# Bucketed attention and a gated product: queries and keys split to float16 in token order and turned by DMA, in place of TensorE transposes and float32r scores

## The chip, the cores and the metric

The kernel runs on one core of one Trainium2 chip. The metric is device time in microseconds (us): the median of the runs of one launch. A core has TensorE (PE; its weight loads are listed as PEld), VectorE (DVE), ScalarE (ACT), GpSimd (POOL) and SyncE (SP), which here only issues DMAs, all on one queue. The hash, score and product matmuls accumulate in PSUM.

## The reference, cut to what matters

```python
batch, n_heads, seq, head_dim = (4, 8, 768, 64)
...
q_bits = (np.einsum('bhsd,dk->bhsk', q, proj) > 0).astype(np.int64)
k_bits = (np.einsum('bhsd,dk->bhsk', k, proj) > 0).astype(np.int64)
powers = 2 ** np.arange(n_bits)
q_bucket = np.sum(q_bits * powers, axis=-1)
k_bucket = np.sum(k_bits * powers, axis=-1)
mask = q_bucket[:, :, :, None] == k_bucket[:, :, None, :]
scores = scale * np.matmul(q, k.transpose(0, 1, 3, 2))
scores = np.where(mask, scores, -1000000000.0)
...
x = np.ascontiguousarray(attn_out.transpose(0, 2, 1, 3)).reshape(B * S, H * D)
...
a = x @ w_a
b = x @ w_b
return (a * b @ w_out).astype(np.float32)
```

Each query and key is hashed to 6 bits by the signs of its products with `proj`; a query sees only the keys of its own bucket of 64. After softmax and the product with v, the heads are laid side by side as x (3072 x 512), which goes through w_a and w_b (512 x 1536 each) and w_out (1536 x 512). The weights arrive as float64, the rest as float32.

## The kernel before, in words

**Work.** There are 4 batches, each of 3 chunks of 256 queries and 2 halves of 4 heads: 24 score units of 8 tiles. A tile is 128 queries of one head against all 768 keys. `qtile` (line 730) makes a tile: scores on TensorE (L740), the maximum on VectorE (L752), a bias (L759), the exponential on ScalarE (L767), a float16 high part of the weights of attention by a cast (L776 on ScalarE for the first eight tiles, L781 on VectorE after), the low part by a subtraction on GpSimd (L786), a DMA transpose of both parts at once (L792), and 18 small matmuls with the high and low parts of v (L801). `su_end` divides by the sums and transposes the unit into the float16 pair xT. `moe` (line 858) takes a chunk of 256 tokens through w_a and w_b (L885: high and low float16 parts, three products), multiplies the two (L899, L907, L914, L917) and runs w_out in float32r (L927); its result is stored at L944.

**Keys and queries.** `kprep` (line 519) loads a pair of heads with tokens and heads interleaved in pieces of 256 bytes (L530), transposes six blocks of 128 x 128 on TensorE (L539), and evicts each head's 64 rows as float32r: high part by ScalarE (L548), a copy of it by GpSimd (L555), low part by VectorE (L560). `bit_rows` (L513) then multiplies by the six hash columns, in two passes for the first batch. The signs become bits (L581, L595), a matmul (L604) turns bits into a distance from each of the 64 buckets, and ScalarE writes a penalty into the 64 unused rows (L613). `qprep` (line 620) does the same for 4 heads of a chunk of queries (L630, L644, L654, L659, L664, L513, L683, L696, L705, L714), with a one-hot row in place of the penalty. So 128 rows hold 64 of data and 64 of marks, and two products a tile give high x high with the mask, and the crossed terms with the low parts.

**Weights.** `to_f32` (line 342) loads a piece of 128 x 512 float64 numbers as pairs of 32-bit words, scales the exponent of the upper word and takes the top byte of the lower one on ScalarE (L355, L363), and joins them to float32 on VectorE (L370). `w_group` (line 377) does so for the four pieces of 512 columns of w_a or w_b (6 groups), takes their common maximum (L400), makes a power of two of it (`scale_of`, L312 to L329), and splits into float16 high (L420, ScalarE) and low (L425, VectorE). `wo_piece` (line 431) does the 12 pieces of w_out (L436, L439). Pieces land in buffers that w_out's products take later.

**Order.** Nothing runs in the order of the source. Every operation is put into a list with its engine, a duration, a key (when it is due, counted in tiles) and the buffers it uses; `Plan.issue` (line 141) then walks through a modelled time and gives each engine the ready operation with the least key whose buffers are free. What comes out is a fixed order for each engine and for SyncE's queue, with waits between them. Keys come from constants: `K0`, `V0`, `Q0`, `WG0`, `WO0`, `M0` for the first batch, weights and first two chunks of the product, `K_LEAD`, `Q_LEAD`, `V_LEAD`, `M_LAG` for the rest.

## Time and profile before

| | |
|---|---|
| median of 3 runs | 1012.9 us (1012.79 to 1012.94) |
| span of the profiled execution | 1010.4 us; its own time is not given beside it, and the medians of the runs lie 2.5 us above |
| TensorE, VectorE, ScalarE, GpSimd busy | 936.4, 630.5, 557.5, 456.2 us |
| DMA | 127.46 MB moved, its queue busy 54.9% of the span |
| chain that ended last | TensorE 86%, VectorE 7%, ScalarE 3% |

The span runs from the first to the last instruction. A busy TensorE is not one at its peak, since matmuls overlap and their ends are modelled; so where matmuls are packed, their cost is read from the start of one group to the start of the next. A row of the groups gives line, engine, operation, written and read tiles, shapes and count, then busy us and mean ns, then idle us before it and what ended that.

### The profile page before, as it was taken

How to read it: one execution, taken by the hardware profiler on the slowest of the kernel's cores; microseconds unless marked ns; L12 is line 12 of the kernel's file. 1: busy time of each engine (PE TensorE's matmuls, PEld its weight loads, DVE VectorE, ACT ScalarE, POOL GpSimd, SP SyncE). 2: the span in 40 equal slices, each digit the busy share in tenths (PEclk: the TensorE clock that was granted, in tenths of full speed). 3: DMA queues.
4: the chain of work that ended last, by engine and by line, in shares of the span. 5: the costliest groups of instructions: out<-in, count | busy, mean ns of one | idle time of the engine just before them, and what ended most of it. 6: DMA issues, size and time to landing. Idle time of an engine off the chain costs nothing.

```text
span 1010.4 us, 22786 instructions
## 1 busy us (share of the span) xinstructions
PE 936.4 (93%) x9132; PEld 793.3 (79%) x9132; DVE 630.5 (62%) x1135; ACT 557.5 (55%) x1067; POOL 456.2 (45%) x372
## 2 busy tenths in 40 slices
PE   3464679999999999999999999999999999999998
...
GB/s 286 223 213 208 188 127 139 123 165 149 102 124 116 105 101 131 110 131 152 119 128 106 105 127 109 108 149 137 126 123 103 105 133 103 95 101 95 32 22 21
DMA packets 370154, 127.46 MB, mean 126 GB/s; under 512 B 353920, under 2 KB 362368, under 8 KB 370048
## 3 DMA queue, kind: packets, MB, share of 16 engines
q1 hardware_dynamic: 370048, 126.00, 54.9%
...
## 4 chain that ended last, share of the span: by engine, by line
PE 86%; DVE 7%; ACT 3%; issue 2%; DMA 1%; SPq 0%; POOL 0%; POOLq 0%; DVEq 0%; ACTq 0%
PE ab L885 37%; PE o L927 19%; PE s L740 13%; PE av L801 9%; PE kb L513 2%; PE qb L513 2%; DVE mx L752 1%; PE pk L539 1%; PE px L837 1%; PE pq L644 1%; ACT e L767 1%; DVE wab L370 1%; DVE wab L425 1%; DVE trk L560 1%; PE ko L604 1%
## 5 line engine op out<-in xcount | busy, mean ns | idle before, releaser
L786 POOL TENSOR_TENSOR a<-e,a 128x768 f16<-128x768 f32 x192 | 323.2, 1683 | 322.0 <-DVE a L781 175.9
L885 PE MATMUL ab<-xT,wab 128*128 128x256 f16 x3456 | 413.3, 273 | 0.5 <-DVE bias L759 0.5
L885 PEld LDWEIGHTS <-wab 128*128 128x128 f16 x3456 | 326.4, 98 | 59.4 <-issue 23.3
L767 ACT ACTIVATE e<-s,bias 128x768 f32<-128x768 f32 x192 | 172.7, 899 | 136.5 <-DVE bias L759 125.1
L927 PE MATMUL o<-wo,g 128*128 128x512 f32 x864 | 234.3, 406 | 0.3 <-ACT g L914 0.2
L752 DVE TENSOR_REDUCE mx<-s 128x1 f32<-128x768 f32 x192 | 182.5, 951 | 70.1 <-PE s L740 69.2
L917 POOL TENSOR_TENSOR g<-g,g 128x256 fp32r<-128x256 f32 x144 | 109.0, 757 | 186.1 <-ACT g L914 175.2
L740 PE MATMUL s<-trk,trq 128*128 128x384 f32 x768 | 180.5, 365 | 7.8 <-ACT e L767 6.3
L927 PEld LDWEIGHTS o<-wo,g 128*128 128x128 f32 x864 | 153.4, 189 | 27.6 <-ACT g L914 0.7
L907 DVE SCALAR_TENSOR_TENSOR g<-ab,absc,a 128x256 f32<-128x256 f32 x144 | 69.4, 482 | 158.8 <-ACT a L899 147.1
L801 PEld LDWEIGHTS <-at 128*128 128x128 f16 x3456 | 122.7, 100 | 32.7 <-issue 24.0
L740 PEld LDWEIGHTS s<-trk,trq 128*128 128x128 f32 x768 | 135.5, 198 | 15.7 <-ACT e L767 10.5
L899 ACT ACTIVATE a<-ab,absc 128x256 f32<-128x256 f32 x144 | 68.3, 474 | 131.0 <-PE ab L885 129.9
L801 PE MATMUL av<-vh,at 128*128 128x64 f16 x2304 | 133.8, 196 | 4.8 <-DMA at<-a 4.8
L781 DVE CAST a<-e 128x768 f16<-128x768 f32 x184 | 111.5, 606 | 25.7 <-ACT e L767 19.6
L914 ACT CAST g<-g 128x256 fp32r<-128x256 f32 x144 | 58.1, 404 | 55.9 <-DVE g L907 54.1
L801 PE MATMUL av<-vl,at 128*128 128x64 f16 x1152 | 66.6, 195 | 1.8 <-DVE vl L499 1.8
L714 ACT ACTIVATE trq<-qo,csb 64x512 fp32r<-64x512 f32 x48 | 32.8, 683 | 35.4 <-PE qo L705 34.9
L664 DVE TENSOR_TENSOR trq<-pq,trq 64x512 fp32r<-64x512 f32 x48 | 33.0, 688 | 24.2 <-ACT trq L659 20.7
L555 POOL CAST trk<-trk 64x768 fp32r<-64x768 f32 x32 | 26.7, 833 | 40.3 <-ACT trk L548 39.4
L560 DVE SCALAR_TENSOR_TENSOR trk<-pk,trk 64x768 fp32r<-64x768 f32 x32 | 30.6, 955 | 21.7 <-ACT trk L548 21.2
L654 ACT CAST trq<-pq 64x512 fp32r<-64x512 f32 x48 | 27.8, 580 | 23.0 <-PE pq L644 20.0
...
## 6 DMA issues: line engine op xcount, KB each, us to landing
...
```

The source lines that it names most:

```text
L740: nc.tensor.matmul(ps.t[:, jj, :HALF], lhsT=trq.t[:, j, i, t * P : (t + 1) * P], rhs=tr.t[:, i, jj * HALF : (jj + 1) * HALF], start=i == 0 ...
L752: lambda: nc.vector.tensor_reduce(out=mx.t[:, u : u + 1], in_=halves(ps.t), axis=AX.XY, op=ALU.max, negate=True),
L767: lambda: nc.scalar.activation(flat2(e.t), halves(ps.t), AF.Exp, bias=bias.t[:, u : u + 1], scale=1.0, accum_out=sm.t[:, u : u + 1],),
L781: "DVE", 0.55, lambda: nc.vector.tensor_copy(out=a2.t[:, 0], in_=e.t), key,
L786: lambda: nc.gpsimd.tensor_tensor(out=a2.t[:, 1], in0=e.t, in1=a2.t[:, 0], op=ALU.subtract),
L801: nc.tensor.matmul(av.t[:, u, :], lhsT=at.t[:, a + kt, :], rhs=w.t[:, h, kt, :], start=i == 0, stop=i == 3 * NT - 1,)
L885: nc.tensor.matmul(pl.t[:, m, :CH], lhsT=wt(m, wi, cc, f), rhs=xi.t[:, cc, :], start=i == 0, stop=i == 3 * NC - 1,)
L899: lambda a=a, pl=pl, gr=gr: nc.scalar.activation(a.t, pl.t[:, 0, :CH], AF.Copy, scale=absc[:, b, gr : gr + 1]),
L907: lambda a=a, g32=g32, pl=pl, gr=gr: nc.vector.scalar_tensor_tensor(out=g32.t, in0=pl.t[:, 1, :CH], scalar=absc[:, b, gr + 1 : gr + 2], in ...
L914: op("ACT", 0.41, lambda g=g, g32=g32: nc.scalar.copy(out=g[0].t, in_=g32.t), kf - 8, r=[g32], w=[g[0], "order_g0"])
L917: lambda g=g, g32=g32: nc.gpsimd.tensor_tensor(out=g[1].t, in0=g32.t, in1=f32(g[0].t), op=ALU.subtract),
L927: nc.tensor.matmul(po.t[:, u, :], lhsT=g[gi].t[:, us], rhs=wo[f].t[:, wi * DM : (wi + 1) * DM], start=f == 0 and i == 0, stop=f == NF - 1 ...
```

## The change

- **Queries and keys stay in token order.** A key unit is a pair of heads in 12 blocks of 128 tokens, a query unit a whole chunk of all 8 heads in 16 blocks. `split` makes a float16 high part (ScalarE), a copy (GpSimd) and a low part (VectorE) beside each other in blocks of 128 x 128: B holds high and low, A holds high and, later, marks. Both are scaled by a power of two: the keys by one for the batch (`k_scale`, which loads all keys of the batch once more, except in the first), the queries by one a chunk for each partition.
- **Turning.** `turn` transposes B and then A, by DMA transposes on SyncE's queue; for the first batch's keys and its first chunk of queries by TensorE, with an eviction on ScalarE (B) or VectorE (A).
- **Hash.** `buckets` multiplies each turned block of B, as the weight, by 12 columns (high and low parts of `proj`), so the bits of a token lie in one partition. VectorE adds the parts, tests the sign, sums to a bucket number, and compares it with 0 to 63 for the marks in A. A second buffer of A does not exist (nA has one, nB two).
- **Scores** are four float16 matmuls of 384 columns. The exponential's scale undoes the powers of two, so a second small VectorE operation a tile sets it (`affine`). Every third tile of a unit is cast on ScalarE.
- **Weights.** The maximum is taken over the upper words as they land, the scale goes into ScalarE's `Prelu`, the high part is a plain copy, and the low parts of the weights and of w_out move from VectorE to GpSimd.
- **Plan.** New constants; four buffers in place of two for the attention weights before and after their transpose; a key and value pair of the first batch is loaded once, into buffers that are used for other things later; buffers of some kinds are now taken in the order in which they were made (`IN_TURN`).

The diff, cut to its core:

```diff
-NE, NA, NAT, NO = 3, 2, 2, 2
...
+NE, NA, NAT, NO, NRAW = 3, 4, 4, 2, 2
...
+ACT_CASTS = 8.63
+CAST_EVERY = 3
+K_LEAD, KS_LEAD, Q_LEAD, V_LEAD = 16.63, 10.65, 7.77, -17.89
+M_LAG = 6.32
+KS0 = -2.53
+K0 = [-63.42, -14.05, -9.5, 14.86]
+V0 = [-11.8, -2.03, 6.24, -14.06]
+Q0 = [-60.96, 10.19, 23.45]
+VS0 = -1.83
+WG0 = [3.31, -0.76, 4.06, 8.52, 14.53, 16.59]
+WO0 = [14.19, 25.61, 30.83]
+M0 = [20.43, -64.42]
+M0_PACE = [2.33, 2.19]
+NBLK = NH * TPC
+HOT = 65504.0
...
         fq, m = g // 2, g % 2
-        zs = []
+        raws = []
+        mx = buf("wmx", [P, NC + 1], F32, f"wmx{g}")
         for cc in range(NC):
             k = g * NC + cc
-            if k + 1 < NPC:
-                tok = ("W", k + 1)
-                z = lambda k=k: wab[:, k + 1, :]
+            src = (w_a, w_b)[m][cc * P : (cc + 1) * P, fq * WP : (fq + 1) * WP]
+            raw = words(src, NF - NSTG + k % NSTG, f"w{k}", key + 0.5 * cc)
+            raws.append(raw)
+            op(
+                "DVE", 0.6,
+                lambda raw=raw, cc=cc: nc.vector.tensor_reduce(
+                    out=mx.t[:, cc + 1 : cc + 2], in_=raw.t[:, :, 1].bitcast(F32), axis=AX.X, op=ALU.max,
+                    apply_absolute_value=True,
+                ),
+                key + 0.5 * cc, r=[raw], w=[(mx, cc)],
+            )
+        key += 0.5 * NC
+        op(
+            "DVE", 0.15,
+            lambda: nc.vector.tensor_reduce(out=mx.t[:, 0:1], in_=mx.t[:, 1:], axis=AX.X, op=ALU.max),
+            key, r=[(mx, cc) for cc in range(NC)], w=[mx],
+        )
+        sc = buf("wsc", [P, 1], F32, f"wsc{g}")
+        w_scale(mx, sc, winv[:, g : g + 1], ("winv", g), f"w{g}", key)
...
+            to_f32(raw, NF - NSTG + k % NSTG, key, z, [tok], sc, [sc, (mx, cc)])
             hi, lo = wab16[:, k, :WP], wab16[:, k, WP:]
             op(
-                "ACT", 0.74,
-                lambda hi=hi, z=z: nc.scalar.activation(hi, z(), AF.Copy, scale=sc.t),
-                key, r=[ztok, sc], w=[("W", k)],
-            )
-            op(
-                "DVE", 0.75,
-                lambda hi=hi, lo=lo, z=z: nc.vector.scalar_tensor_tensor(
-                    out=lo, in0=z(), scalar=sc.t, in1=hi, op0=ALU.mult, op1=ALU.subtract
-                ),
...
-            "DVE", 0.7,
-            lambda: nc.vector.tensor_tensor(
+            "POOL", 1.15,
+            lambda: nc.gpsimd.tensor_tensor(
                 out=wo[f].t[:, DM:], in0=y.t, in1=f32(wo[f].t[:, :DM]), op=ALU.subtract
             ),
-            key, r=[y, (wo[f], 0)], w=[(wo[f], 1)], sbuf=True,
-        )
...
+    HOME0 = [(f"wo{i}", 1, cp) for i in range(4)] + [("a2", NA, p2)] * 2 + [("at", NAT, p2)] * 2
...
+    def k_scale(b, key):
+        ksc[b] = buf("ks", [P, 1], F32, f"ks{b}")
+        largest(
+            k, b, ksc[b], kinv[:, b : b + 1], ("kinv", b), f"k{b}", key,
+            None if b else k0, least=1.0, top=QK,
+        )
...
+    def buckets(tB, n, pw, a, op_eq, value, name, key, tag):
+        ps = psum(f"b_{name}", tag)
+        def rows():
+            for u in range(n):
                 nc.tensor.matmul(
-                    out[:m], lhsT=pjw[:, w0 + lo : w0 + lo + m], rhs=rhs,
-                    start=i == 0, stop=i == len(groups) * len(passes) - 1,
+                    ps.t[:, 0, u * 2 * NBITS : (u + 1) * 2 * NBITS], lhsT=tB.t[:, u, :],
+                    rhs=pw.rearrange("p a b -> p (a b)"), start=True, stop=True,
                 )
-                i += 1
+        op("PE", 0.03 * n, rows, key, r=[tB, "pjk", "pjq"], w=[ps])
+        sums = buf("b_sum", [P, NBITS * NBLK], F32, f"bs_{name}")
+        code = buf("b_code", [P, NBLK, 2], F16, f"bc_{name}")
+        def codes():
+            s = sums.t[:, : NBITS * n]
+            nc.vector.tensor_reduce(
+                out=s, in_=ps.t[:, 0, : 2 * NBITS * n].rearrange("p (a b) -> p a b", b=2),
+                axis=AX.X, op=ALU.add,
+            )
+            nc.vector.scalar_tensor_tensor(
+                out=s, in0=s, scalar=0.0, in1=powers[:, : NBITS * n], op0=ALU.is_gt, op1=ALU.mult
+            )
+            with nc.allow_low_precision("whole numbers up to 63"):
+                nc.vector.tensor_reduce(
+                    out=code.t[:, :n],
+                    in_=s.rearrange("p (u i) -> p u i", i=NBITS).unsqueeze(2).to_broadcast([P, n, 2, NBITS]),
+                    axis=AX.X, op=ALU.add,
+                )
+        op("DVE", 0.7, codes, key, r=[ps, "cw"], w=[sums, code])
+        def marks():
+            x = a.t[:, :n, D:].rearrange("p u (a b) -> p u a b", b=2)
+            nc.vector.tensor_tensor(
+                out=x, in0=code.t[:, :n].unsqueeze(2).to_broadcast([P, n, NBUCK // 2, 2]),
+                in1=iota.unsqueeze(1).to_broadcast([P, n, NBUCK // 2, 2]), op=op_eq,
+            )
+            nc.vector.tensor_scalar(
+                out=a.t[:, :n, D:], in0=a.t[:, :n, D:], scalar1=value, scalar2=None, op0=ALU.mult
+            )
+        op("DVE", 0.09 * n, marks, key, r=[code, "cw"], w=[(a, "mark")], sbuf=True)
...
+    def turn(src, n, dst, key, toks, name, evict=None):
+        if evict is None:
+            op(
+                "SP", T_ISSUE * n / 12,
+                lambda: nc.sync.dma_start_transpose(
+                    out=dst.t, in_=src.t[:, :n].rearrange("p u x -> p (u x)")
+                ),
+                key, r=toks, w=[dst], svc=2.2 * n / 12,
+            )
+            return
+        ps = psum(f"t_{name}_{evict}", "o" if evict == "ACT" else "s")
+        def blocks():
+            out = ps.t.rearrange("p a b -> p (a b)").bitcast(F16)
+            for u in range(n):
+                nc.tensor.transpose(out=out[:, u * P : (u + 1) * P], in_=src.t[:, u, :], identity=ident16)
+        op("PE", 0.11 * n, blocks, key, r=[*toks, "cw"], w=[ps], hold=[dst])
+        def copy():
+            in_ = ps.t.rearrange("p a b -> p (a b)").bitcast(F16)[:, : n * P]
+            out = dst.t.rearrange("p u x -> p (u x)")
+            if evict == "ACT":
+                nc.scalar.copy(out=out, in_=in_)
+            else:
+                nc.vector.tensor_copy(out=out, in_=in_)
...
+    def split(raw, n, sc, rtoks, A, B, hi_at, name, key):
+        x = raw.t.rearrange("p h t d -> p (h t) d")
+        lo_at = D - hi_at
+        def part(y, at):
+            return y.t[:, :n, at : at + D]
+        op(
+            "ACT", 0.23 + 0.058 * n,
+            lambda: nc.scalar.activation(part(B, hi_at), x, AF.Copy, scale=sc.t), key, r=[raw, *rtoks],
+            w=[(B, "hi")],
+        )
+        op(
+            "POOL", 0.1 + 0.065 * n,
+            lambda: nc.gpsimd.tensor_copy(out=part(A, 0), in_=part(B, hi_at)), key, r=[(B, "hi")],
+            w=[(A, "hi")],
+        )
+        op(
+            "DVE", 0.1 + 0.08 * n,
+            lambda: nc.vector.scalar_tensor_tensor(
+                out=part(B, lo_at), in0=x, scalar=sc.t, in1=part(B, hi_at), op0=ALU.mult, op1=ALU.subtract
+            ),
+            key, r=[raw, *rtoks, (B, "hi")], w=[(B, "lo")], sbuf=True,
+        )
+    def natural(name):
+        return [buf(f"n{x}", [P, NBLK, P], F16, f"n{x}_{name}", n) for x, n in (("A", 1), ("B", 2))]
...
+        n = f"k{b}_{hp}"
+        A, B = natural(n)
+        tA, tB = kT[b, hp] = [buf(f"kT{x}", [P, 2 * NT, P], F16, f"kT{x}_{n}", NPAIR) for x in "AB"]
+        raw = load_pair(k, b, hp, f"rk_{n}", key - 1, hold=[tA, tB]) if b else k0[hp]
+        split(raw, 2 * NT, ksc[b], [ksc[b]], A, B, 0, n, key)
+        turn(B, 2 * NT, tB, key, [(B, "hi"), (B, "lo")], n, None if b else "ACT")
+        buckets(tB, 2 * NT, pjk, A, ALU.not_equal, -HOT, n, key, tag)
+        turn(A, 2 * NT, tA, key, [(A, "hi"), (A, "mark")], n, None if b else "DVE")
...
+        n = f"q{b}_{c}"
+        raw = buf("raw", [P, NH, TPC, D], F32, f"rq_{n}", NRAW)
+        sig = buf("q_sig", [P, 1], F32, f"qsig_{n}")
+        tA, tB = [buf(f"qT{x}", [P, NBLK, P], F16, f"qT{x}_{n}") for x in "AB"]
+        qT[b, c] = tA, tB, sig
+        op(
+            "SP", DMA_ISSUE,
+            lambda: nc.sync.dma_start(
+                out=raw.t,
+                in_=q[b].rearrange("h (p t) d -> p h t d", t=NT)[:, :, c * TPC : (c + 1) * TPC, :],
+            ),
+            key - 1, w=[raw], svc=1.8, hold=qT[b, c][:2],
+        )
+        A, B = natural(n)
+        mx = buf("q_mx", [P, 1], F32, f"qmx_{n}")
...
+        split(raw, NBLK, sc, [sc], A, B, D, n, key)
+        turn(B, NBLK, tB, key, [(B, "hi"), (B, "lo")], n, None if b or c else "ACT")
+        buckets(tB, NBLK, pjq, A, ALU.is_equal, HOT, n, key, tag)
+        turn(A, NBLK, tA, key, [(A, "hi"), (A, "mark")], n, None if b or c else "DVE")
...
         def scores():
-            for i in range(2):
+            for i, (x, y) in enumerate(((qA, kA), (qB, kB))):
                 for jj in range(2):
                     nc.tensor.matmul(
-                        ps.t[:, jj, :HALF], lhsT=trq.t[:, j, i, t * P : (t + 1) * P],
-                        rhs=tr.t[:, i, jj * HALF : (jj + 1) * HALF], start=i == 0, stop=i == 1,
+                        ps.t[:, jj, :HALF], lhsT=x.t[:, uq, :],
+                        rhs=y.t[:, h * NT + jj * 3 : h * NT + jj * 3 + 3, :].rearrange("p t x -> p (t x)"),
+                        start=i == 0, stop=i == 1,
                     )
         op(
-            "PE", 0.72, scores, key, w=[ps],
-            r=[(trq, x) for x in ("hi", "hi2", "lo", "hot")] + [(tr, x) for x in ("hi", "hi2", "lo", "pen")],
-        )
-        mx, bias, sm, av = st["mx"], st["bias"], st["sm"], st["av"]
+            "PE", 0.66, scores, key, w=[ps, "order_s"], r=[qA, qB, kA, kB],
+        )
...
+        def affine():
+            col = slice(u, u + 1)
+            nc.vector.tensor_scalar(
+                out=width.t[:, col], in0=mx.t[:, col], scalar1=NONE, scalar2=sig.t, op0=ALU.is_lt, op1=ALU.mult
+            )
+            nc.vector.tensor_scalar(
+                out=bias.t[:, col], in0=mx.t[:, col], scalar1=width.t[:, col], scalar2=LN_ESC,
+                op0=ALU.mult, op1=ALU.add,
+            )
+        op("DVE", 0.32, affine, key - 0.5, r=[(mx, u), sig], w=[(bias, u)])
...
+        if key < ACT_CASTS or u % CAST_EVERY == 0:
+            op("ACT", 0.83, lambda: nc.scalar.copy(out=a2.t[:, 0], in_=e.t), key, r=[e], w=[(a2, 0), "casts"])
         else:
             op(
                 "DVE", 0.55, lambda: nc.vector.tensor_copy(out=a2.t[:, 0], in_=e.t), key,
-                r=[e, "casts"], w=[(a2, 0)], sbuf=True,
+                r=[e], w=[(a2, 0), "casts"], sbuf=True,
             )
...
-            qprep(b, c, half, start - Q_LEAD if b else Q0[i], tag)
+            if half == 0:
+                qprep(b, c, start - Q_LEAD if b else Q0[c], tag)
...
```

459 lines of the change are left out of this document (159 added, 300 removed).

## The prediction

> **What bounds the kernel now.** I read the page first: shares of the engines, then the 40 slices of about 25 us.
>
> ```profile
> PE 936.4 (93%) x9132; PEld 793.3 (79%) x9132; DVE 630.5 (62%) x1135; ACT 557.5 (55%) x1067; POOL 456.2 (45%) x372
> ...
> PE   3464679999999999999999999999999999999998
> ```
>
> From the seventh slice to the last, TensorE is full; only the first six slices are not. So there are two regimes, and the table of stretches gives each its numbers (columns: stretch, length, busy us of PE, PEld, DVE, ACT, POOL with counts, granted clock, DMA share, GB/s).
>
> ```profile
> 0.00:50.00 50.00, 19.04 (x64) 10.48 (x65) 28.75 (x46) 33.73 (x52) 5.15 (x10) 0.93 0.75 257
> 50.00:100.00 50.00, 27.78 (x182) 20.44 (x182) 46.41 (x74) 43.00 (x72) 16.51 (x10) 0.60 0.88 209
> 100.00:150.00 50.00, 34.87 (x310) 27.43 (x309) 45.46 (x79) 38.91 (x71) 20.47 (x11) 0.75 0.72 157
> ...
> 150.00:300.00 150.00, 149.22 (x1538) 128.63 (x1537) 112.26 (x194) 86.54 (x168) 80.05 (x64) 1.00 0.63 137
> ...
> 750.00:900.00 150.00, 150.00 (x1548) 130.32 (x1547) 87.79 (x169) 78.46 (x162) 76.01 (x60) 1.00 0.50 107
> ```
>
> Until 150 us VectorE is the fullest compute engine: 46.4 and 45.5 us of 50 in the second and third stretch, with ScalarE (43.0) and the DMA (0.88) close behind; TensorE waits, and its granted clock falls to 0.60. After 150 us TensorE has no gap to speak of (149.2 of 150, then 150.0), and no other engine is above three quarters. Every microsecond of TensorE work taken out after 150 us therefore shortens the run, until another resource fills up. Before 150 us TensorE's work is worth little, and VectorE's is worth most.
>
> **Part one: TensorE work after 150 us.** Prices come from the timeline of TensorE, as start of a group to start of the next, since the matmuls are packed.
>
> ```profile
> 230.49 0.34 PE L801 MATMUL av<-vh,at 128*128 128x64 f16 x6
> ...
> 231.01 0.85 PE L539 MATMUL pk<-csb,rk 128*128 128x128 f32 x6
> 231.62 1.64 PE L927 MATMUL o<-wo,g 128*128 128x512 f32 x6
> ...
> 236.18 0.94 PE L740 MATMUL s<-trk,trq 128*128 128x384 f32 x4
> 236.96 0.86 PE L513 MATMUL kb<-trk,pjw 128*56 128x384 f32 x4
> 237.66 1.55 PE L927 MATMUL o<-wo,g 128*128 128x512 f32 x6
> ...
> 240.90 0.49 PE L604 MATMUL ko<-bits_k,wbit 128*128 128x384 f16 x2
> 241.22 1.47 PE L885 MATMUL ab<-xT,wab 128*128 128x256 f16 x12
> ```
>
> ```profile
> 562.63 0.63 PE L644 MATMUL pq<-csb,rq 128*128 128x128 f32 x4
> 563.02 0.94 PE L740 MATMUL s<-trk,trq 128*128 128x384 f32 x4
> ...
> 568.43 0.63 PE L513 MATMUL qb<-trq,pjw 128*56 128x256 f32 x4
> 568.90 0.87 PE L740 MATMUL s<-trk,trq 128*128 128x384 f32 x4
> ```
>
> The counts in this regime, from the groups of the window 150 to 1011 us:
>
> ```profile
> L740 PE MATMUL s<-trk,trq 128*128 128x384 f32 x680 | 151.4, 350 | 0.1
> ...
> L644 PE MATMUL pq<-csb,rq 128*128 128x128 f32 x80 | 12.2, 275 | 0.0
> L513 PE MATMUL kb<-trk,pjw 128*56 128x384 f32 x48 | 10.7, 345 | 0.0
> ```
>
> Removed, a pair of key heads: six transposes 0.61 us (231.01 to 231.62), hash rows 0.70 (236.96 to 237.66), penalty matmuls 0.32 (240.90 to 241.22), together 1.63; 48 hash matmuls in fours are 12 pairs, so 19.6 us. Removed, a query unit: transposes 0.39 (562.63 to 563.02) and hash rows 0.47 (568.43 to 568.90); its two penalty matmuls are 256 wide, two thirds of the 0.32 above, so 0.21: together 1.07. 80 transposes in fours are 20 units: 21.4 us.
>
> Scores: four matmuls of 384 columns in float32r take 0.78 us (236.18 to 236.96), 195 ns each. The same width with a float16 128x128 weight is in this trace: two take 0.32 us, 160 ns each. So a tile of four falls by at most 0.14 us. Where eight scores run together the change of type costs less, so I take 0.11 a tile; 170 tiles give 18.7 us (24 at most, 12 if it is 0.07).
>
> Added: the new hash matmuls in float16, a 128x128 weight and 12 columns each. 12 pairs of 12 and 10 query chunks of 16 are 304. The nearest row is the attention output: 18 matmuls of 64 columns, each with its own weight, from 230.49 to 231.01, 29 ns each: 8.8 us. If the columns ruled it would be 1.5 us (12 of 384 columns at 160 ns), and 49 if a small matmul cost as much as a whole 384-wide one; 9 is taken, since the load of a weight is the same. The scale of the keys adds three short broadcasts, 1 us at most. The Trainium skill, page "TensorE: Matmul & The Clock Gate", section "Back-to-back issue gap", budgets about 81 ns for each weight load with a matmul even at 128 columns; by it the 304 would take an estimated 25 us and the time would be 16 us longer, but the trace's 29 ns for the same pair speaks against it.
>
> Sum: 19.6 + 21.4 + 18.7 - 8.8 - 1 = 50 us less TensorE work after 150 us.
>
> **What could take TensorE's place there.** VectorE is at 112.3 of 150 us in the fullest stretch. A batch loses the key and query evictions and bit tests and 18 of 48 casts, and gains splits, codes, marks, maxima and a second small operation a tile; with the prices below that is near balance, and on 140 us instead of 150 it stays under 85%. The DMA:
>
> ```profile
> L792 SPq DMA_TRANSPOSE at<-a x192: 1273/1405/3378, 58.9 to 937.1; - x192
> ```
>
> 192 transposes now; 12 key pairs with two like them and 11 query chunks with two a third larger add the worth of 53, 28%. Were the DMA share of 0.63 all transposes, it would become 0.81; less, as the loads in small pieces go. SyncE issues one in 1.4 us. I charge 2 us for waits, 0 to 8.
>
> **Part two: the start.** VectorE's groups in the window 0 to 150 us, out of 120.6 us busy (28.75 + 46.41 + 45.46):
>
> ```profile
> L752 DVE TENSOR_REDUCE mx<-s 128x1 f32<-128x768 f32 x22 | 20.9, 949 | 2.2 <-PE s L740 1.9
> L370 DVE SCALAR_TENSOR_TENSOR wab<-raw_w 128x512 int32<-128x512 int32 x23 | 19.4, 858 | 3.6 <-ACT raw_w L363 3.6
> L425 DVE SCALAR_TENSOR_TENSOR wab<-wab,wsc 128x512 f16<-128x512 f32 x20 | 17.0, 851 | 0.3 <-ACT wab L420 0.2
> L400 DVE TENSOR_REDUCE wmx<-wab 128x1 f32<-128x2048 f32 x5 | 11.4, 2278 | 0.1
> L560 DVE SCALAR_TENSOR_TENSOR trk<-pk,trk 64x768 fp32r<-64x768 f32 x8 | 7.6, 955 | 8.3 <-ACT trk L548 8.2
> L781 DVE CAST a<-e 128x768 f16<-128x768 f32 x12 | 6.6, 546 | 0.0
> L664 DVE TENSOR_TENSOR trq<-pq,trq 64x512 fp32r<-64x512 f32 x8 | 5.5, 687 | 3.4 <-ACT trq L659 2.9 <-ACT trq L654 0.4
> L439 DVE TENSOR_TENSOR wo<-wo_y,wo 128x512 fp32r<-128x512 f32 x8 | 5.4, 682 | 0.2 <-ACT wo L436 0.2
> L499 DVE SCALAR_TENSOR_TENSOR vl<-vr,vs,vh 128x768 f16<-128x768 f32 x4 | 4.0, 1010 | 0.0
> L581 DVE TENSOR_SCALAR bits_k<-kb 24x768 f16<-24x768 f32 x4 | 3.8, 945 | 4.3 <-PE kb L513 4.3
> ...
> L759 DVE TENSOR_SCALAR bias<-mx 128x1 f32<-128x1 f32 x22 | 3.3, 149 | 0.5
> ```
>
> Gone from VectorE: the low parts of the weights (17.0) and of w_out (5.4), which go to GpSimd; the maximum of the assembled weights (11.4); the key and query low parts (7.6 and 5.5): 46.9. Added: 24 maxima over 512 raw words, 0.68 each by the slope between 768 (949 ns) and 2048 (2278), 16.3; four key maxima at 0.95, 3.8; two query scales, 1024 wide, 1.2 and three small operations of 0.15, 3.3; low parts of four key pairs at 1.01 and two query chunks at 1.3, 6.6; six sets of codes, three short operations of some 0.3, 5.4; marks, two passes over 768 or 1024 16-bit values, each between half and the whole of 0.95 for 768: 1.2 and 1.6 taken, 8.0; five evictions of 1536 to 2048 16-bit values, between 0.95 and 1.8, 1.4 taken, 7.0; the second small operation of 22 tiles, 3.3; some 25 other small ones, 3.8. Together 57.5, ends 50 and 63: 11 more. The old bit tests of the keys (3.8) go as well, and three eighths of the casts (6.6) go to ScalarE, 2.5: 4 us more in all, ends -3 and 10.
>
> GpSimd, at 42.1 us of 150 (5.15 + 16.51 + 20.47), gets 36 subtractions of 512 columns. Its subtraction of 768 takes 1.68 us, so 1.1 each, 40 us in all, nearly twice the work, and that collides:
>
> ```profile
> L786 POOL TENSOR_TENSOR a<-e,a 128x768 f16<-128x768 f32 x192 | 323.2, 1683 | 322.0 <-DVE a L781 175.9
> ```
>
> ```profile
> L370 DVE SCALAR_TENSOR_TENSOR wab<-raw_w x23: 671/682/2129, 13.3 to 148.6; 128x512 int32<-128x512 int32 x23
> ```
>
> The median of this VectorE operation (the second row: least, median and longest ns) is 682 ns, the mean 858, the longest 2129: now and then it waits out something. 23 times the difference of 0.176 is 4 us; with GpSimd twice as busy I charge 4 us more.
>
> Against that stands idle time: 29.4 us of 150, 21.3 of it in the first 50, while the keys go in series through five engines to the first scores.
>
> ```profile
> 3.71 3.32 DMA rk<-in_k_dram
> ...
> 51.86 2.94 PE s L740 x8
> ```
>
> That chain stays serial: the new kernel has one buffer for the turned-in half with the marks (nA), so key and query units follow one another, an estimated 12 us each (nine steps of about 1.3 us, as the operations above last). The first keys land at 7 us today (3.71 + 3.32); all four pairs, with their scale, should be there by 14, and one key pair and one query chunk then give first scores near 40. But the raw maxima need only their piece of weight to land, so VectorE has work from the first landing; I expect 10 us idle to remain, 19 less. ScalarE loses four evictions a key pair and six a query unit, and is no longer close. The first batch's keys and its first query chunk are turned by TensorE, 128 float16 transposes; they cost nothing while TensorE waits there, and at the 0.1 us of the old ones (0.61 for six) 13 us if that cover were gone.
>
> The start: 4 + 4 - 19 = 11 us shorter. Ends: 35 shorter, if attention and the first weight groups come out earlier together, and 15 longer.
>
> **Sum.** The profiled execution spans 1010.4 us; 1010.4 - 50 - 11 + 2 = 951.4. The median of the runs, 1012.9, is 2.5 above the span, whose own time is not given separately: 953.9, so 954 us.
>
> **The rivals.** (1) The start does not shrink: the weights' landing rules it (DMA 0.75, 0.88, 0.72 above; the weights' bytes stay), or the words lose as much as the idle time gives back: 1010.4 - 50 + 2 + 2.5 = 965. For it, the 0.88; against it, that VectorE is fuller. (2) GpSimd blocks VectorE. Some 45 operations in the start read two operands from SBUF (33 words, 6 low parts of keys and queries, 4 of values, others); if each waited half of the longest extra, 0.72 us (2129 less 682, halved), that is 32 us in place of the 8 charged, and the time is 978. The page "SBUF — State Buffer" of the Trainium skill, section "Who interferes with whom", says that a VectorE instruction with two SBUF inputs and a GpSimd one that reads SBUF exclude each other for the whole of an instruction; the 2129 agrees with it, the median of 682 shows that it seldom strikes today. (3) The start shrinks by 35 to 40: 925 to 930. TensorE could fill by 115 us if VectorE's work were spread evenly; against it, ScalarE and the DMA are each over 38 us of 50 too. (4) The scores do not run at the penalty matmul's pace: 18.7 us come back, 973. Against it are the two ko rows themselves. (5) Slower: SyncE's queue is in order. A turn of keys that waits for marks holds the attention transposes behind it, and TensorE, in order too, stands at the attention output. With four buffers in place of two for those transposes it takes a long hold; if each of the 46 turns cost TensorE more than (50 + 11) / 46 = 1.3 us the gain is gone, and at 2 us the time is 954 + 92 = 1046. TensorE's gapless 750 us show no such wait today.
>
> **Chances.** Forecast, 938 to 963: 0.46. (1) 0.17, (2) 0.08, (3) 0.16, (4) 0.04, (5) 0.06, no net change 0.01, and other gains 0.02. The range takes (1) to (4): 922 to 982. A measurement of this kernel can tell about 0.2% from no change. Faster 0.93, same 0.01, slower 0.06.
>
> **What would show it.** Right: TensorE gapless from about 140 us on; scores of four in 0.64 to 0.70 us; new hash groups of 12 in about 0.35 us; first scores near 40 us; VectorE over 90% from 20 to 140 us. Wrong: waits of the attention output on its transpose after 150 us (rival 5), words with a mean over 1.1 us (rival 2), hash matmuls of 80 ns, or a start as long as before.

## The result, and the profile after

The changed kernel takes 966.25 us (median of 4 runs, 966.06 to 966.76) against 1012.85 for the kernel before (4 runs): ratio 0.9547, interval 0.9534 to 0.9561. A later set of 3 rounds on another chip gave 966.27 and 0.9549 (0.9535 to 0.9564). The forecast was 954.0, in a range of 922 to 982; the time lies 12 us above the forecast, above the 938 to 963 that went with it, and beside rival (1), the start that does not shrink (965), which the range took in. The profiled execution spans 965.0 us, against 1010.4.

The first page, shares of the engines and the 40 slices (24 us each):

```profile
PE 877.3 (91%) x9182; PEld 709.2 (73%) x9182; DVE 707.8 (73%) x1422; ACT 506.4 (52%) x931; POOL 516.5 (54%) x404
...
PE   3654369999989999999999999999999999999998
...
DVE  7999999998789877569886656679885665475211
```

TensorE has lost 59 us of busy time and VectorE has gained 77. TensorE's line is the old one: six or seven slices in which it waits, then full. VectorE's is at 9 from the second slice to the ninth.

The table of stretches, the start and then the rest (columns as before: stretch, length, busy us of PE, PEld, DVE, ACT, POOL, granted clock, DMA share, GB/s):

```profile
0.00:50.00 50.00, 23.64 (x216) 18.00 (x217) 43.32 (x95) 30.05 (x39) 8.84 (x11) 0.87 0.68 233
50.00:100.00 50.00, 23.00 (x226) 16.04 (x225) 48.45 (x97) 40.41 (x68) 36.06 (x23) 0.60 0.85 217
100.00:150.00 50.00, 28.97 (x263) 20.78 (x264) 47.79 (x90) 32.79 (x59) 35.12 (x25) 0.67 0.83 218
```

```profile
150.00:180.00 30.00, 26.07 (x297) 20.84 (x296) 29.37 (x47) 22.90 (x43) 23.77 (x18) 1.00 0.78 148
```

```profile
200.00:300.00 100.00, 96.19 (x1035) 77.80 (x1033) 86.72 (x173) 50.95 (x95) 55.86 (x44) 0.98 1.04 208
300.00:450.00 150.00, 150.00 (x1640) 123.17 (x1639) 113.08 (x239) 76.23 (x145) 79.63 (x65) 1.00 0.88 170
```

VectorE is busy 139.6 of the first 150 us (it was 120.6), so the idle time there is almost gone, and yet TensorE is not full until some 180 us: it is busy 26 of the 30 us from 150 to 180. After that it is full again, but for 3.8 us between 200 and 300.

**Where the 45.4 us come from.** Counting score tiles, attention outputs and product matmuls that TensorE has behind it at 180 us, the two kernels are level: 29 tiles, 24 outputs, 144 matmuls of `ab` and 30 of `o` before; 29, 25, 154 and 30 after. What remained then took 1010.4 - 180 = 830.4 us before and 965.0 - 180 = 785.0 after, a difference of 45.4. So the whole gain is made after 180 us, and the start gives none (the one output and ten matmuls more are under 2 us). The gain after 180 us, by kind, adds up from the start of each matmul on TensorE's timeline to the start of the next, without the idle time (us; some 4 us behind TensorE's last matmul are in neither column):

| from 180 us on | before | after |
|---|---|---|
| keys: transposes, hash rows, penalties | 19.3 | none |
| queries: the same | 23.3 | none |
| new hash matmuls (288) | none | 7.5 |
| scores (651 and 652 matmuls) | 122.9 | 104.5 |
| `o`, the w_out product (834 and 834) | 204.7 | 208.3 |
| `ab`, attention output, `px`, broadcasts | 454.8 | 455.4 |
| idle | 1.0 | 4.7 |

These rows of TensorE's timeline after show two of the prices:

```profile
321.28 0.49 PE L781 MATMUL s<-kTA_k,qTA_q 128*128 128x384 f16 x2
321.60 0.49 PE L781 MATMUL s<-kTB_k,qTB_q 128*128 128x384 f16 x2
321.93 0.34 PE L846 MATMUL av<-vh,at 128*128 128x64 f16 x6
```

A tile of four scores takes 321.93 - 321.28 = 0.65 us, where the rows of the prediction had 0.78.

### The profile page after: what moved, and what is told of

It is laid out like the page before. It is cut to its first block, busy times and chain, and to the rows that moved or that the text cites. A ratio compares the mean times of both kernels' runs of the same rounds, so it can differ in the third digit from the quotient of the medians.

```text
span 965.0 us, 22855 instructions
## 1 busy us (share of the span) xinstructions
PE 877.3 (91%) x9182; PEld 709.2 (73%) x9182; DVE 707.8 (73%) x1422; ACT 506.4 (52%) x931; POOL 516.5 (54%) x404
## 4 chain that ended last, share of the span: by engine, by line
PE 76%; DVE 19%; issue 2%; ACT 1%; DMA 1%; SPq 0%; POOLq 0%; DVEq 0%; POOL 0%; ACTq 0%
PE ab L930 36%; PE o L972 19%; PE s L781 11%; PE av L846 9%; DVE mx L793 3%; DVE wab L399 2%; DVE wmx L461 1%; DVE a L826 1%; PE px L882 1%; DVE wo_y L399 1%; DVE nB_k L690 1%; DVE width L803 1%; DVE bias L806 1%; DVE nA_k L625 1%; DMA k0m<-in_k_dram 1%
## 5 line engine op out<-in xcount | busy, mean ns | idle before, releaser
L815 ACT ACTIVATE e<-s,bias,width 128x768 f32<-128x768 f32 x192 | 190.2, 990 | 203.2 <-DVE bias L806 183.7
L846 PEld LDWEIGHTS <-at 128*128 128x128 f16 x3456 | 129.0, 101 | 34.1 <-issue 19.2
L826 DVE CAST a<-e 128x768 f16<-128x768 f32 x115 | 81.4, 711 | 55.2 <-ACT e L815 54.8
L781 PE MATMUL s<-kTA_k,qTA_q 128*128 128x384 f16 x384 | 100.4, 345 | 21.8 <-ACT e L815 12.8
L781 PE MATMUL s<-kTB_k,qTB_q 128*128 128x384 f16 x384 | 99.8, 344 | 0.0
L823 ACT CAST a<-e 128x768 f16<-128x768 f32 x77 | 64.0, 831 | 1.8
L781 PEld LDWEIGHTS <-qTA_q 128*128 128x128 f16 x384 | 29.5, 101 | 46.7 <-issue 40.0
L781 PEld LDWEIGHTS <-qTB_q 128*128 128x128 f16 x384 | 39.3, 102 | 28.7 <-issue 6.2
L806 DVE TENSOR_SCALAR bias<-mx,width 128x1 f32<-128x1 f32 x192 | 41.1, 214 | 6.8
L803 DVE TENSOR_SCALAR width<-mx,qsig_q 128x1 f32<-128x1 f32 x192 | 40.6, 211 | 5.1
```

Of the source, the lines that this page charges most:

```text
L781: nc.tensor.matmul(ps.t[:, jj, :HALF], lhsT=x.t[:, uq, :], rhs=y.t[:, h * NT + jj * 3 : h * NT + jj * 3 + 3, :].rearrange("p t x -> p (t x)"),
L815: lambda: nc.scalar.activation(flat2(e.t), halves(ps.t), AF.Exp, bias=bias.t[:, u : u + 1], scale=width.t[:, u : u + 1], accum_out=sm.t[:, ...
L823: op("ACT", 0.83, lambda: nc.scalar.copy(out=a2.t[:, 0], in_=e.t), key, r=[e], w=[(a2, 0), "casts"])
L826: "DVE", 0.55, lambda: nc.vector.tensor_copy(out=a2.t[:, 0], in_=e.t), key,
L846: nc.tensor.matmul(av.t[:, u, :], lhsT=at.t[:, a + kt, :], rhs=w.t[:, h, kt, :], start=i == 0, stop=i == 3 * NT - 1,)
```

## The experiments

Runs of different calls were on different chips, on which the kernel before took 1008.4 to 1012.9 us. So each experiment is given as a ratio to the kernel before on its own chip, and where it is set against the changed kernel, the ratios are compared (0.001 is 1 us). All but the three of one set of rounds are single runs. Four runs of the changed kernel on one chip spread over 2.3 us and seven of the kernel before over 3.2, so 2 or 3 thousandths between single runs say little.

**1. What filled VectorE in the start.** My theory after the result: GpSimd's 36 low parts shut VectorE out, so that VectorE's operations there last longer. The rival: there is simply too much work on VectorE, whatever GpSimd does. Three kernels, one edit each against the changed one. The first leaves out the low parts of w_a and w_b:

```diff
-                lambda hi=hi, lo=lo, z=z: nc.gpsimd.tensor_tensor(out=lo, in0=z(), in1=hi, op=ALU.subtract),
+                lambda hi=hi, lo=lo, z=z: nc.gpsimd.memset(lo, 0.0),
```

> The changed kernel, but GpSimd fills the low parts of w_a and w_b with zeros in place of subtracting (24 operations that read nothing; the order of the work is the same, and the low parts of these weights are left out). Theory: VectorE sets the length of the start, and GpSimd's subtractions stretch it: in the changed kernel's first 150 us the 22 word operations run 1004 ns against a median of 686 (7 us lost), the eight low parts of keys and values 1.36 against 1.01 us (3 us), the marks' second pass 0.90 against 0.36 to 0.43 (3 us). Then some 8 to 14 us go: 952 to 958 us. Rival, the landing of the weights sets the start and VectorE is only full beside it: 964 to 967 us.

Measured: 958.9 us, ratio 0.9483, 6.4 thousandths below the changed kernel: a little short of the 8 to 14 us that were expected but clear of the rival's 964 to 967, though every load of the weights is still there. The gain is made in the start: at 180 us this kernel has 31 tiles, 27 outputs, 188 matmuls of `ab` and 36 of `o` behind it, some 7 us of TensorE work more than the changed one. The second takes the raw maxima over 8 words of 512 (so the scale of a weight group does not see the rest):

```diff
-                    out=mx.t[:, cc + 1 : cc + 2], in_=raw.t[:, :, 1].bitcast(F32), axis=AX.X, op=ALU.max,
+                    out=mx.t[:, cc + 1 : cc + 2], in_=raw.t[:, :8, 1].bitcast(F32), axis=AX.X, op=ALU.max,
```

> The changed kernel, but the 24 maxima over the weights' raw words look at 8 words of 512 (so the power of two comes from a part of the weights; the order of the work is the same). VectorE loses about 12 us of work in the first 150 us (24 times 0.67 down to some 0.17 us). Theory, VectorE sets the length of the start: 10 to 13 us shorter, 953 to 956 us. Rival, the landing of the weights: 964 to 967 us.

Measured: 963.2 us, ratio 0.9526, only 2.1 thousandths, where 10 to 13 us were expected; that is hardly clear of the spread. The third gives VectorE the low parts back:

```diff
-                "POOL", 1.15,
-                lambda hi=hi, lo=lo, z=z: nc.gpsimd.tensor_tensor(out=lo, in0=z(), in1=hi, op=ALU.subtract),
+                "DVE", 0.75,
+                lambda hi=hi, lo=lo, z=z: nc.vector.tensor_tensor(out=lo, in0=z(), in1=hi, op=ALU.subtract),
...
-            "POOL", 1.15,
-            lambda: nc.gpsimd.tensor_tensor(
+            "DVE", 0.7,
+            lambda: nc.vector.tensor_tensor(
```

> The changed kernel with the low parts of w_a, w_b and w_out back on VectorE, where they were before (24 at about 0.74 and 12 at 0.68 us: 26 us more, some 21 of them in the first 150 us), in the order that the planner then gives. Theory, VectorE's load sets the start, less some 10 us that GpSimd no longer takes from it: 974 to 980 us. Rival, exclusion by GpSimd was the main loss: 956 to 966 us.

Measured: 988.0 us, ratio 0.9771, so 22 thousandths worse, and slower than the 974 to 980 expected. What it does to the duration of one operation is seen in the view of one line's instructions, L399, the word-joining operation on VectorE, with least, median and longest ns; first the changed kernel, then this one.

```profile
L399 DVE SCALAR_TENSOR_TENSOR wab<-raw_w x22: 678/686/2136, 46.8 to 141.9; 128x512 int32<-128x512 int32 x22
L399 DVE SCALAR_TENSOR_TENSOR wo_y<-raw_wo x12: 679/1186/2140, 73.9 to 189.1; 128x512 int32<-128x512 int32 x12
```

```profile
L399 DVE SCALAR_TENSOR_TENSOR wo_y<-raw_wo x12: 679/684/1964, 93.0 to 189.8; 128x512 int32<-128x512 int32 x12
```

The pieces of w_out have a median of 1186 ns while GpSimd makes low parts, and 684 when it doesn't. The 22 pieces of w_a and w_b keep their median, but their mean falls from 1004 ns to 833 in `no_pool_low`. So the shutting out is real. The Trainium skill, page "SBUF — State Buffer", section "Who interferes with whom", calls the shared port pair of VectorE and GpSimd an exclusive lock; a median that moves while the least time stays agrees with it. But holding VectorE up costs less than giving it the work: with the subtractions on VectorE the start is longer still, and TensorE is short of work until 450 us (87.3 of 100 and 144.3 of 150):

```profile
200.00:300.00 100.00, 87.28 (x862) 68.81 (x861) 84.39 (x160) 44.62 (x82) 44.35 (x37) 0.97 0.95 196
300.00:450.00 150.00, 144.30 (x1562) 117.61 (x1562) 104.84 (x211) 73.65 (x141) 80.92 (x63) 0.97 0.85 158
```

The second run, which gained next to nothing, says that VectorE's work is not all that counts. With maxima over 8 words in place of 512, VectorE's busy time in the first 150 us fell only from 139.6 to 132.7, and those 7 us are idle time now, most of it in the first and the third stretch:

```profile
0.00:50.00 50.00, 25.40 (x220) 19.20 (x221) 39.96 (x102) 31.68 (x42) 9.09 (x12) 1.00 0.72 243
...
100.00:150.00 50.00, 32.72 (x306) 23.43 (x307) 44.78 (x94) 32.73 (x58) 34.51 (x26) 0.70 0.84 211
```

**2. The types alone.** Float16 queries, keys and hash weight in the kernel *before*, with nothing else of the change:

```diff
-BIG = float(2.0**60)
+BIG = float(2.0**13)
...
-        tr = [buf("trk", [P, 2, S], F32R, f"trk_{n}_{h}", NH) for h in range(2)]
+        tr = [buf("trk", [P, 2, S], F16, f"trk_{n}_{h}", NH) for h in range(2)]
...
-        trq = [buf("trq", [P, 2, 2, CH], F32R, f"trq_{n}_{h}", 4) for h in range(2)]
+        trq = [buf("trq", [P, 2, 2, CH], F16, f"trq_{n}_{h}", 4) for h in range(2)]
```

> The kernel before, with its query and key tiles and the hash weight in float16 in place of float32r, everything else as it was (no scaling, and one float16 part where there were float32r bits, so the numbers are coarser). It does the type change alone. Four scores should take 0.65 us in place of 0.76 (170 tiles after 150 us: 18 us), four hash matmuls 0.65 in place of 0.70 for keys and 0.43 in place of 0.47 for queries (1 us): 990 to 995 us. If the slower pace came from the other things in the score matmuls and not from the type: 1009 to 1012 us.

Measured: 1000.3 us, ratio 0.9919, a gain of 8, less than the 18 and more that was expected. The timelines show why; first the kernel before, then this one:

```profile
420.47 0.86 PE L740 MATMUL s<-trk,trq 128*128 128x384 f32 x4
421.17 0.35 PE L801 MATMUL av<-vh,at 128*128 128x64 f16 x6
...
426.27 0.96 PE L740 MATMUL s<-trk,trq 128*128 128x384 f32 x4
427.07 2.79 PE L885 MATMUL ab<-xT,wab 128*128 128x256 f16 x24
```

```profile
408.36 1.46 PE L740 MATMUL s<-trk,trq 128*128 128x384 f16 x8
409.66 0.34 PE L801 MATMUL av<-vh,at 128*128 128x64 f16 x6
...
414.21 0.82 PE L740 MATMUL s<-trk,trq 128*128 128x384 f16 x4
414.87 0.34 PE L801 MATMUL av<-vh,at 128*128 128x64 f16 x6
```

Eight scores now take 1.30 us, 163 ns each, which is the expected pace. But what a tile took before depends on what stands ahead of it. The one at 426.27 stands behind the attention output, float16, and takes 0.80 us. The one at 420.47 stands behind a group of `o`, float32r like itself, and takes 0.70. The float16 tile at 414.21 stands behind `o` too and takes 0.66. So a tile behind `o` or behind hash rows (41 of 137 groups of scores after 180 us) has little to save.

By the rows the scores still save what was expected, 19.8 us, and `o` loses 4.6 (204.7 to 209.3). But some of this only moves a border between rows. Behind float16 scores the first matmul of `o` takes 366 ns, against 230 behind float32r ones, but the last score ahead of it is followed after 28 ns in place of 162. The pair of four scores and six of `o` takes 2.06 us here and 2.17 before, so `o` pays nothing there. In the same way a float32r tile behind `ab` showed a high price while it cut the last matmul of `ab` short, by 81 ns at each of 37 places, and `ab` has these back now. Without the two the scores save some 14 us. The hash rows, which were to save 1 us, take 1.2 more. With the same number of matmuls of each kind, TensorE's work after 180 us falls by 8 us, which is the gain.

**3. Turning by TensorE, and the buffers.** All key units and the marks of all query units turned by TensorE, the rest as changed (464 more float16 transposes, with their evictions):

```diff
-        turn(B, 2 * NT, tB, key, [(B, "hi"), (B, "lo")], n, None if b else "ACT")
+        turn(B, 2 * NT, tB, key, [(B, "hi"), (B, "lo")], n, "ACT", "s" if b else "o")
...
-        turn(A, 2 * NT, tA, key, [(A, "hi"), (A, "mark")], n, None if b else "DVE")
+        turn(A, 2 * NT, tA, key, [(A, "hi"), (A, "mark")], n, "DVE", "s")
...
-        turn(A, NBLK, tA, key, [(A, "hi"), (A, "mark")], n, None if b or c else "DVE")
+        turn(A, NBLK, tA, key, [(A, "hi"), (A, "mark")], n, "DVE", "s")
```

> The changed kernel, with all key turns and the query marks' turns of the later batches by TensorE too (464 more float16 transposes of 128 x 128, evicted by ScalarE and VectorE); the query data's turns stay with the DMA. At half the 108 ns of a 256-column float16 matmul, 54 ns each, 25 us more TensorE work, all of it after 150 us where TensorE has no gap; the DMA loses 36 of its 46 turns. Theory, the DMA's turns are worth what TensorE's would cost, and their DMA time costs nothing: 988 to 996 us. Rival, the DMA near 0.9 busy holds TensorE back by itself: under 980 us.

Measured: 1016.8 us, ratio 1.0083: more than the whole gain is gone, 54 thousandths, twice what was expected. The 432 transposes that run after 180 us explain 26 us of it, 60 ns each in the mean and 56 in this row (16 from 336.01 to 336.91):

```profile
336.01 1.06 PE L654 MATMUL t_q_DVE<-cw,nA_q 128*128 128x128 f16 x16
336.91 1.47 PE L930 MATMUL ab<-xT,wab 128*128 128x256 f16 x12
```

The rest is in the stretches of the same kernel:

```profile
200.00:300.00 100.00, 90.60 (x932) 73.66 (x931) 79.39 (x150) 43.13 (x77) 41.90 (x35) 0.97 0.81 180
300.00:450.00 150.00, 142.45 (x1587) 116.04 (x1583) 105.15 (x209) 74.30 (x138) 79.68 (x62) 0.98 0.68 124
```

TensorE is short of work by 9.4 us between 200 and 300 and by 7.6 between 300 and 450. Counted as in the table above, what follows 180 us takes 50.0 us more than in the changed kernel: 26 for the transposes, 15 more of idle time (20.1 against 4.7) and 9 in the other groups. The added evictions lie on VectorE and ScalarE, and the turned blocks pass through the scores' PSUM buffers; which of the two makes the idle time, this run does not tell apart. So turning by DMA, which raises the DMA share from 0.68 to 0.88 in the stretch from 300 to 450, is worth more here than the kernel's whole gain.

Rival (5) held that those turns would make the attention transposes wait. The changed kernel has four buffers on either side of them; this one has two:

```diff
-NE, NA, NAT, NO, NRAW = 3, 4, 4, 2, 2
+NE, NA, NAT, NO, NRAW = 3, 2, 2, 2, 2
```

> The changed kernel with two buffers, as before, in place of four for the attention weights ahead of and behind their transpose. The DMA is busy 0.85 to 0.90 after 300 us where it was 0.5 to 0.6. If the two extra buffers carry the longer way through a fuller queue (4.0 us to landing against 3.2), TensorE waits at the attention output: 975 to 1000 us. If they carry nothing: 964 to 968 us.

Measured: 1021.6 us, ratio 1.0103, slower than the kernel before and than the 975 to 1000 expected. Its worst stretch:

```profile
300.00:450.00 150.00, 137.44 (x1455) 108.84 (x1455) 102.31 (x212) 71.34 (x136) 76.28 (x59) 0.91 0.76 137
```

TensorE's waits after 150 us (engine, line, waited for: us, times, longest) in this kernel:

```profile
PE s L781 <- ACT e L815: 16.2, 11, 3.2
PE av L846 <- DMA at<-a: 5.3, 6, 1.6
```

and the same view of the changed kernel:

```profile
PE ab L930 <- DVE g L952: 3.7, 4, 1.8
PE s L781 <- ACT e L815: 1.4, 2, 1.2
PE av L846 <- DMA at<-a: 1.3, 1, 1.3
```

With four buffers the wait for the transpose falls from 5.3 us to 1.3, and the wait of the scores, which cannot go on while the tiles behind them stand, from 16.2 to 1.4. In all, TensorE sits idle for 32.0 us after 180 us in place of 4.7; another 11 us are work that this kernel has not done by 180 us and the changed one has, and some 16 us are the same matmuls taking longer, in stretches where the granted clock is lower (0.91 from 300 to 450). So the buffers are worth the whole gain. That the turns are to blame, as rival (5) held, is not shown: the longest wait of SyncE's queue in this kernel is that of the transposes (L837) for the attention output, which must free a buffer, 178.0 us in 92 waits, and in the changed kernel no such wait stands among the longest. The kernel before, with two buffers as well, has that wait too (187.8 us) and stays full; there a transpose lands after 3.2 us in the median, here after 4.0.

**4. A faster start that was given back.** If VectorE is the bound of the start, moving work off it should shorten the run. The first batch's key marks and its first query chunk's, scaled and evicted by ScalarE in one operation:

```diff
+            if hot is not None:
+                nc.scalar.activation(out, in_, AF.Copy, scale=hot)
...
-        buckets(tB, 2 * NT, pjk, A, ALU.not_equal, -HOT, n, key, tag)
-        turn(A, 2 * NT, tA, key, [(A, "hi"), (A, "mark")], n, None if b else "DVE")
+        buckets(tB, 2 * NT, pjk, A, ALU.not_equal, -HOT, n, key, tag, b > 0)
+        turn(A, 2 * NT, tA, key, [(A, "hi"), (A, "mark")], n, *((None,) if b else ("ACT", hot_k, -HOT)))
```

> The changed kernel, with the first batch's marks scaled to their value by ScalarE as it evicts the turned blocks, in place of a pass of VectorE before and an eviction by VectorE after: VectorE loses five passes (some 4 us) and five evictions (5 us) in the first 50 us, ScalarE gains 8 us. Theory, VectorE's amount of work sets the start: 956 to 959 us. Rival, what sets it is the order in which the engines were planned to wait for one another, so work taken away in the first 50 us leaves idle time there: 963 to 967 us.

and the same with the casts of the first twenty tiles on ScalarE (`ACT_CASTS` 20.63 for 8.63):

> As marks_on_scalar, and ScalarE also makes the float16 high part of the attention weights for all tiles due before 20.63 in place of 8.63 (some 8 casts of 0.7 us leave VectorE between 50 and 150 us, where it is busy 0.96). Theory, VectorE's amount of work sets the start: 950 to 956 us. Rival, the planned order: 961 to 967 us; ScalarE becoming the bound (0.81 busy from 50 to 100 us): over 968 us.

Measured: 971.1 (0.9630) and 972.0 (0.9639): both lost 8 to 9 thousandths, where the theory had a gain. The second lies where ScalarE as the new bound was expected (over 968), but ScalarE is busy only 42.7 and 43.7 of 50 us from 50 to 150. Yet the start did get faster: at 180 us the first of them has 32 tiles, 28 attention outputs, 210 matmuls of `ab` and 42 of `o` behind it, against 29, 25, 154 and 30, some 12 us of TensorE work ahead. The stretches from 260 to 300 us show it being lost; the changed kernel first, then `marks_on_scalar`:

```profile
260.00:280.00 20.00, 19.25 (x193) 15.52 (x191) 17.88 (x36) 11.78 (x23) 11.80 (x9) 1.00 1.07 201
280.00:300.00 20.00, 16.93 (x191) 12.55 (x190) 19.10 (x35) 10.93 (x20) 12.41 (x9) 0.91 1.04 217
```

```profile
260.00:280.00 20.00, 14.60 (x146) 10.34 (x145) 16.90 (x32) 8.33 (x15) 9.46 (x7) 0.81 0.84 201
280.00:300.00 20.00, 15.80 (x155) 11.04 (x155) 18.57 (x37) 11.60 (x21) 11.02 (x7) 0.68 1.15 209
```

Here the second batch of keys comes in. TensorE has used up the product work that it could do, sits idle for 9.6 of 40 us, and its granted clock falls to 0.68, so that what it does takes longer: a matmul of the attention output starts every 53 ns at 281 to 282 us, in a piece at a granted clock of 0.5, and every 29 at 1.0. In `marks_and_casts` that stretch is no worse than in the changed kernel (19.60 and 16.18); there the time goes in smaller pieces, and its cause was not followed up. Nor is every head start lost: `no_pool_low` kept its 7 us.

A guess at the cause: the loads and maxima of batches to come crowd this stretch. Two kernels hold them back until the second query chunk of the batch ahead of them, the changed kernel and the one with the marks, and a third repeats the changed kernel, with 3 rounds each:

```diff
-            t = load_pair(src, b, hp, f"{name}m_{hp}", key, home=None if keep is None else HOME0[first + hp])
+            t = load_pair(
+                src, b, hp, f"{name}m_{hp}", key, home=None if keep is None else HOME0[first + hp],
+                after=[("gate", b)] if b >= 2 else (),
+            )
...
+            "PE", 0.66, scores, key, w=[ps, "order_s", *([("gate", b + 1)] if (c, half, u) == (1, 0, 0) else ())],
```

> The changed kernel once more, as the yardstick on this chip for the two that follow: a ratio to the kernel before of 0.953 to 0.956.

> The changed kernel, but the loads for the maxima of keys and values of batches 2 and 3 may not start until the batch ahead is in its second chunk of queries. In the changed kernel those of batch 2 are loaded between 245 and 270 us, when the DMA is over 1.0 busy and the third and fourth key pair of batch 1 wait for the same two load buffers; TensorE then stands for some 4 us from 260 to 300 us and its clock falls to 0.91. Theory, these early loads hold up the keys: 3 to 6 us shorter, ratio 0.948 to 0.951. Rival, the key units are held by their own serial chain: ratio 0.953 to 0.957.

> marks_on_scalar and late_maxima together. marks_on_scalar was about 12 us ahead of the changed kernel in work done at 180 us (32 score tiles, 210 first-product and 42 second-product matmuls against 29, 154 and 30) and lost 12 us of TensorE between 200 and 300 us, where the maxima of batch 2 were loaded from 221 us on. Theory, VectorE's work sets the start and the early loads took the gain back: ratio 0.940 to 0.947. Rival, the gain of the start is given back at the keys of batch 1 whatever the loads do: ratio 0.953 to 0.962.

Measured: 966.3, 968.7 (0.9568, 0.9552 to 0.9584) and 971.7 us (0.9598, 0.9583 to 0.9612). The guess fell: nothing was gained, and the stretch from 260 to 300 was no better in the last of them (13.46 and 14.80 of 20). What the trace of `late_maxima` shows instead are the key units one after another on SyncE's queue:

```profile
262.49 1.79 SPq L646 DMA_TRANSPOSE kTB_k<-nB_k  x1
273.85 1.44 SPq L646 DMA_TRANSPOSE kTA_k<-nA_k  x1
275.38 1.76 SPq L646 DMA_TRANSPOSE kTB_k<-nB_k  x1
292.81 1.49 SPq L646 DMA_TRANSPOSE kTA_k<-nA_k  x1
```

These are the batch's third and fourth unit: from the turn of B to that of A, with hash, codes and marks between, it is 11 and 17 us, and the fourth cannot be scored before 293 us. The last run takes just that away, from the kernel with the marks on ScalarE: the hash, codes and marks of the second batch's keys are left out.

```diff
+        if b == 1:
+            op(
+                "DVE", 0.3, lambda: nc.vector.memset(A.t[:, : 2 * NT, D:], 0.0), key, r=[(B, "lo"), (A, "hi")], w=[(A, "mark")]
+            )
+        else:
+            buckets(tB, 2 * NT, pjk, A, ALU.not_equal, -HOT, n, key, tag, b > 0)
```

> marks_on_scalar with one thing left out besides: the hash, the codes and the marks of the second batch's four key units (their marks are zeros, so a quarter of the masks is wrong). In marks_on_scalar TensorE was some 12 us of work ahead at 180 us and gave it back between 260 and 300 us (14.6 and 15.8 of 20 us), while it had run out of product work and VectorE was busy 16.9 and 18.6 of 20 there. Theory: the key units of the second batch, with their serial chain and their work on VectorE, are what it then waits for. With four chains shortened by some 5 us each and about 10 us less VectorE work, TensorE should be above 18 of 20 us in both stretches, and the time 959 to 965 against the 971.1 of marks_on_scalar. Rival: the tiles themselves (maximum, scale, exponential, one after the other) set the pace there once product work is used up, whatever the keys do: TensorE stays at 14 to 16 of 20, and the time falls only by the 48 hash matmuls, 1.4 us, to 969 to 970.

Measured: 963.1 us, ratio 0.9513, within the theory's 959 to 965; its span is 961.1, 8.0 shorter than that of `marks_on_scalar` (969.1), of which 1.4 are the hash matmuls. But TensorE reached only part of what was expected:

```profile
260.00:280.00 20.00, 16.19 (x158) 11.75 (x156) 18.59 (x36) 11.85 (x21) 13.85 (x11) 0.96 1.13 237
280.00:300.00 20.00, 17.38 (x179) 13.61 (x178) 14.90 (x32) 11.50 (x21) 11.62 (x9) 0.78 1.16 214
```

16.2 and 17.4 of 20, where over 18 was expected. So the key units of the second batch are part of it, 3.2 us of the 9.6 idle in this stretch and more around it; whether by their chain or by their work on VectorE, this run does not tell apart. The waits of `marks_on_scalar` from 255 to 305 us speak for VectorE and for the rival, the pace of the tiles:

```profile
ACT e L824 <- DVE bias L815: 10.2, 9, 2.6
...
PE s L790 <- ACT e L824: 5.4, 3, 2.9
```

TensorE waits there for exponentials that must free a buffer of the scores (with two smaller waits of the same kind, 2.7 and 1.2 us, that is 9.3 of the 9.6) and not once for a turned key; the exponentials wait for the small operations on VectorE, which is busy 35.5 of the 40 us from 260 to 300. How much of VectorE's part there is the keys' is not measured. A fifth pair of buffers for turned keys, which would let the units start earlier, was not tried.

## Why the prediction was right, and where it was not

- **TensorE's work after 150 us: right, in its parts and in its sum.** Predicted 19.6 for keys, measured 19.3; 21.4 and 23.3 for queries; 18.7 and 18.3 for scores; 8.8 against 7.5 for the new hash matmuls. The sum was -50; all of TensorE's groups together fell by 49.3 (825.0 to 775.7, counted from 180 us). `o`, which the change does not touch, shows 3.6 us more, 250 ns each for 245. This is no cost of its own: at the 25 places where `o` follows float16 scores its first matmul takes longer by what the last score loses, 3.3 us in all, as experiment 2 found. So the scores truly save some 15 of the 18.3. Their price before, 195 ns, was that of a tile behind float16 work, and the mean was 189; that the 0.11 a tile, picked between 0.07 and 0.14, came out so well is in part luck.
- **Hash matmuls:** `b_q` takes 25 ns each, by these rows (16 from 372.21 to 372.61), `b_k` 27. The 29 of the attention output was the right neighbour. The Trainium skill, page "TensorE: Matmul & The Clock Gate", section "Back-to-back issue gap", has 81 ns a matmul for a stream of such pairs at 128 columns, and 25 ns as the floor for up to 64 columns of an isolated one; here the stream of 12 columns runs at the floor.

```profile
372.21 0.55 PE L596 MATMUL b_q<-pjq,qTB_q 128*128 128x12 f16 x16
372.61 2.56 PE L930 MATMUL ab<-xT,wab 128*128 128x256 f16 x22
```

- **Waits there: 2 us charged, 3.7 more measured** (4.7 against 1.0), nearly all between 260 and 300 us. Rival (5) did not come: with four buffers the attention output waits once, for 1.3 us. `two_buffers` shows what they are worth, but not that turns are what they cover.
- **The start: the step that failed.** "The start: 4 + 4 - 19 = 11 us shorter" came out near 0, and the prediction's own sign of being wrong, a start as long as before, was there. Of its terms the idle time was exact: 29.4 us of VectorE's 150 before, 150 - 139.6 = 10.4 after, 19 less. The first scores come at 29.5 us, earlier than the 40 that were expected:

```profile
29.46 0.80 PE L781 MATMUL s<-kTA_k,qTA_q 128*128 128x384 f16 x2 [1.12 <-DVE kTA_k L664]
```

But the work rose by 139.6 - 120.6 = 19.0 and not by 4 + 4, and that cancelled the idle time. (Busy and idle time add up to 150, so the two 19s are one number. What makes it a finding is that TensorE stands where it stood at 180 us: VectorE needed 19 us more for the same progress.) The groups of VectorE in the first 150 us show which terms were too small:

```profile
L399 DVE SCALAR_TENSOR_TENSOR wab<-raw_w 128x512 int32<-128x512 int32 x22 | 20.8, 1004 | 0.0
...
L461 DVE TENSOR_REDUCE wmx<-raw_w 128x1 f32<-128x512 f32 x24 | 15.5, 673 | 0.0
L690 DVE SCALAR_TENSOR_TENSOR nB_k<-k0m,ks,nB_k 128x768 f16<-128x768 f32 x4 | 5.4, 1356 | 0.0
...
L806 DVE TENSOR_SCALAR bias<-mx,width 128x1 f32<-128x1 f32 x22 | 4.7, 214 | 0.8
L803 DVE TENSOR_SCALAR width<-mx,qsig_q 128x1 f32<-128x1 f32 x22 | 4.6, 211 | 0.6
...
L629 DVE TENSOR_SCALAR nA_k<-nA_k 128x768 f16<-128x768 f16 x4 | 3.6, 901 | 0.1
L625 DVE TENSOR_TENSOR nA_k<-bc_k,cw 128x768 f16<-128x768 f16 x4 | 3.3, 826 | 0.1
```

The words take 1004 ns in the mean at an unchanged median of 686, where 858 stood before: 3 us. The low parts of the keys take 1356 ns for the 1010 that was taken: 1.4; those of the values lose as much. The two small operations of a tile take 9.3 us together, not 6.6: each reads a scale from memory and takes 0.21 us, where 0.15 was taken. The marks of four key and two query units come to 11.0 for 8.0 (3.6 and 3.3 by the rows of L629 and L625, 4.1 for the queries). Some 3 us are maxima of later units that now come earlier. That makes some 15 us, against the 4 that were charged for GpSimd. The size of each was small; the sum was not. Other terms about cancel: codes 7.2 for 5.4, evictions 5.0 for 7.0, and words of w_out 4.8 where 7.8 stood.
- **The rivals.** (1) gave the time (965). Of its two ways, the landing of the weights is not what held the start, since `no_pool_low` loads the same and gained; the words lost as it said, but only 3 us, and the other small terms did the rest. (2) was half right: GpSimd does shut VectorE out, and taking its low parts of w_a and w_b away gained 6.4 us and not 24. That VectorE's operations are held is shown; that this alone made the start as long as it was is not, since in `no_raw_max` some 7 us of VectorE's time went idle instead. (3) did not come; the one start that was shorter by 12 us, in `marks_on_scalar`, was lost again by 300 us. (Its "over 38 us of 50" does not hold for the DMA in the third stretch, where 0.72 is 36 us.) So the time fell inside the range because the range took rival (1) in, which had a chance of 0.17.
